# A linear-attention block with a low-rank mixer on one core: how the low-rank sum reaches its operand, and when U and V are converted

## The chip, the cores and the metric

The kernel runs as one program on one core of a Trainium2 chip. Times are device microseconds of one execution. Before the change three runs took 656.55, 654.02 and 652.91 us; the median is 654.02.

The engines are called as the profile calls them: PE (TensorE, with PEld for its weight loads), DVE (VectorE), ACT (ScalarE), POOL (GpSimd) and SP (SyncE, which here issues most transfers). Each engine works through its own queue in order.

## The reference, cut to what matters

Inputs q, k, v are [4, 8, 768, 64] (batch, heads, sequence, head width) in float32. U is [768, 32] and V is [32, 768], both float64, so their 64-bit words must be turned into float32 on the chip; the same holds for the two weight matrices (512 x 2048 and 2048 x 512).

```
for each block of the sequence:                      # per head, decay lam
    intra = (q k^T * Dmask) v
    inter = (q * lam_pow) kv_state
    out   = intra + inter
    kv_state = lam_block * kv_state + (k * rev_pow)^T v
x = out, heads side by side                          # [4, 768, 512]
h = x^T @ U @ V                                      # mixing along the sequence, rank 32
u = x + h^T
out = u + relu(u @ w_ch1) @ w_ch2
```

## The kernel before, in words

**The first stage** (about 0 to 115 us) goes through 24 steps, numbered s = 0 to 23: four batches of six blocks of 128 positions. Step s is in batch b = s // 6 at place c = s % 6. "First step" below means c = 0 (steps 6, 12, 18) and "second step" c = 1 (steps 7, 13, 19). In each step PE does, in this order: for step s+1 the transposes of q and k into the bank pqk (L361); the intra product of scores and values into px (L455); the state product into pkv (L427); the inter product into px (L466); and the scores of step s+1 into pss (L408). ACT copies the transposes out as `qt` and `kt` (L367) and px as x_nat (L472); it also scales the old state (faded, L401). DVE multiplies the scores by the decay mask (sm, L417) and forms the new state (kv, L433 to L438). POOL scales q and k (qs L392, ks L381). In steps 6 and 0 to 5 the state product comes ahead of the intra product. Its bank is pm up to step 6, pqk in a first or second step after that, and pss in the other steps: so in a second step it has to wait until ACT has copied `kt` out of pqk, and in the later steps the next scores have to wait until DVE has read pkv.

**The low-rank part.** In the last step of a batch, `low` (L477) multiplies U's transpose by the batch's x, in four column groups of 128, each into its own 32 rows of one bank: pp is [128, 128], 32 rows for each of four groups. The mixing product (`mix`, L567) needs this sum spread: its weights are 64 rows (32 of V's high part, 32 of V's low part) for each half of the columns, and so the moving operand p_hl needs the sum's high part and its low part, each twice, on both sets of 32 rows. V's own high and low parts lie in v_hl. In batches 0 to 2 the sum is taken out of pp as four 32x128 copies (ACT two, L492, and DVE two, L524) into a tile of 32 rows, DVE masks off the low bits (L527), ACT casts the high part to four places (L535, 32x256 each), POOL subtracts for the low part (L539, two of 32x256), and ACT copies that to the other rows (L546, two). These three parts are a list from which `next_of_low` (L550) runs the next one. In the first step of the next batch all three are run: two after the transposes, the third before the products. The last batch has its own form, which the change leaves alone.

From step 7 on, each step also mixes one earlier block (block s - 7; in a second step that is the first block of the batch before): `mix` on PE at the head of the step into the bank pm, `mixed` (L577) on DVE, which adds it to x_nat; SP stores the sum (u_d, L595). One step later `turn` (L597) transposes that block into the other half of pm, and `split` (L643) divides it into a high and a low part, on ACT (L644) and DVE (L645).

**Conversions.** `weight_steps` (L111) loads 64-bit words (L146) and makes float32 of them: `one` is two DVE operations, exponent (L166) and mantissa (L155, which with `apart` becomes a step of its own), and two ACT activations (L173, L174); `two` (L184), `three` (L192) and `four` (L197) are DVE. For weights, `five` is an ACT scaling (L215), `six` (L220) and `seven` (L227) are DVE. V's own last steps (L701) take the high part by a DVE mask (L718) and four ACT casts (L725) and the low part by DVE and POOL (L729). Where these steps run is set by hand, in a table of step numbers (L742); `aside` (L753) runs what the table has for a step, and what ACT has to do for it is run a little later, by `late`. The number NS stands for what is done around the first products of the next stage.

**The head of the products** (about 115 to 142 us): the first units of `hidden` (L823), 24 matmuls of 512 columns for each pair of column groups, with pieces of the last batch's mixing, sums (L575) and transposes (put, L608) put in by count (L892 to L904).

**The rest** (to 649.6 us) is the two large products, with PE in one row.

The order within a step is written out by hand as a list of pieces (L653 to L685); a program keeps that order on each engine and adds the waits.

Of the kernel before, what the change touches and what calls it, by code (L numbers as in the profile page):

```python
# [18 lines left out]
def kernel(  # L19
# [28 lines left out]
    nc = tc.nc  # L48
# [8 lines left out]
    R = moe_U.shape[1]  # L57
    G = P // R
# [45 lines left out]
    def tmp(name):  # L104
        return wconv.tile([P, C], FP32, tag="tmp", bufs=2, name=name)
# [129 lines left out]
    def w1_steps(ft, in_parts=False, apart=False):  # L235
        def tile_of():
            w1v[ft] = w1_pool.tile([P, 3, C], F32R, tag="w1", name="w1")
            return w1v[ft]

        cols = moe_w_ch1[:, ft * P : (ft + 1) * P].rearrange("(c p) f -> p c f", p=P)  # L240
        return split_steps(tile_of, cols, in_parts, apart=apart)
# [230 lines left out]
        nc.scalar.copy(xs[s].rearrange("p (a x e) -> p x a e", a=HP, x=2), px)  # L472
        del st[s]

    pps, others = {}, {}

    def low(b):  # L477

        pp = two_banks("pp", "px")[:, 0, 0:P] if b < B - 1 else bank([P, P], "pp", "b2")
        for c in range(NT):  # L480
            for g in range(G):
                nc.tensor.matmul(  # L482
                    out=pp[g * R : (g + 1) * R, :], lhsT=u_w[:, c, :],
                    rhs=xs[b * NT + c][:, g * P : (g + 1) * P],
                    start=(c == 0), stop=(c == NT - 1),
                )
        if b == B - 1:
            pps[b] = pp
            return
        pps[b] = rows_f = tmp("p_f")[0:R]  # L490
        for g in range(2):
            nc.scalar.copy(rows_f[:, g * P : (g + 1) * P], pp[g * R : (g + 1) * R])  # L492
        others[b] = pp

    def low_rows(b):

        pp, t = pps.pop(b), tmp("p_h")[0:R]
        own = [(slice(g * R, (g + 1) * R), slice(g * P, (g + 1) * P)) for g in range(G)]
        if b == B - 1:
            h, h2, l, l2 = (p_hl[g * R : (g + 1) * R] for g in range(G))  # L500
# [21 lines left out]
        rows_f, pp = pp, others.pop(b)  # L522
        for g in range(2, G):
            nc.vector.tensor_copy(  # L524
                out=rows_f[:, g * P : (g + 1) * P], in_=pp[g * R : (g + 1) * R]
            )
        nc.vector.tensor_scalar(t.bitcast(U32), rows_f.bitcast(U32), HI, None, ALU.bitwise_and)  # L527
        wide = [slice(x * 2 * P, (x + 1) * 2 * P) for x in range(2)]

        def place(g, low):  # L530
            return p_hl[g * R : (g + 1) * R, wide[low]]

        def spread():
            for g in range(G):
                nc.scalar.copy(place(g, 0), t[:, wide[g // 2]])  # L535

        def low_part():
            for x in range(2):
                nc.gpsimd.tensor_tensor(  # L539
                    out=place(2 * x, 1), in0=rows_f[:, wide[x]], in1=t[:, wide[x]],  # L540
                    op=ALU.subtract,
                )

        def spread_low():
            for x in range(2):
                nc.scalar.copy(place(2 * x + 1, 1), place(2 * x, 1).bitcast(FP32))  # L546

        pps[b] = [spread, low_part, spread_low]

    def next_of_low(b):  # L550
        pps[b].pop(0)()
# [102 lines left out]
    for s in range(NS):  # L654
        b, c = divmod(s, NT)
        done = s - NT - 1
        more = s + 1 < NS
        turns = done > 0 and (done - 1) // TG < FG
        mixes = 0 <= done < NS - NT - 1
        rows = c == 0 and b > 0  # L660
        step = [("fade", s)] * (c > 0)
        step += [("mix", done)] * mixes + [("turn", done - 1)] * turns
        step += [("split", done - 1)] * turns
        step += [("prep", s + 1)] * more
        step += [("mix", done + 1)] * (not more)
        step += [("next_of_low", b - 1)] * rows + [("next_of_low", b - 1)] * rows
        step += [("scale", s + 1)] * more
        step += [("mixed", done)] * mixes
        step += [("late", s - 1)] * (1 < s < NT - 1 or s > NT)
        step += [("turned", done - 2)] * (done > 1 and c == 1)  # L670
        step += [("mixed", done + 1)] * (not more)
        step += [("next_of_low", b - 1)] * rows
        both = [("intra", s), ("state", s)]
        step += (both if s > NT else both[::-1]) + [("next_v", s), ("inter", s)]
        step += [("late", s)] * (s < 2 or s in (NT - 1, NT))
        step += [("turned", done - 1)] * (done > 0 and c > 0)
        step += [("scores", s + 1)] * more
# [63 lines left out]
    )  # L741
    side = {}  # L742
    for steps, at in (
        (u_side, (-1, 1, 1, 2, 2)),
        (v_steps(), (0, 0, 3, 3, 4, 4, 4, 5, 5)),
        (w1_steps(0, True), (8, 9, 10, 11, 13, 14, 15, 16, 16, 17, 19)),
        (w1_steps(1, True, True), (15, 16, 17, 18, 20, 20, 21, 22, 23, 23, NS, NS)),
    ):
        assert len(steps) == len(at)
        for step, n in zip(steps, at):  # L750
            side.setdefault(n, []).append(step)

# [22 lines left out]
    load_next("k", nc.scalar)  # L775
    for name in "vkvq":
        load_next(name)
    aside(-1)
    load_next("k")
    make_identity(nc, ident)  # L780
    pl = two_banks("pl", "pss")[:, 0, 0:H]
# [122 lines left out]
        rest.append((unit, i, "turn", c0 + n))  # L904
    run["enter"] = enter_first_product
    head = [(pair, ft) for two in (pairs[:2], pairs[2:]) for ft in (0, 1) for pair in two]
    side = list(zip((0, 0), last)) + list(zip((0, 3, 3, 3, 4, 4, 4, 4), w1_steps(2)))
    for i, (pair, ft) in enumerate(head):
        before = {}
        for unit, n, *piece in rest:  # L910
# [162 lines left out]
```

## Time and profile before

| | |
|---|---|
| median of three runs | 654.02 us |
| the profiled execution | 651.42 us |
| its span, first to last instruction | 649.6 us |
| granted TensorE clock | 1.000 |
| PE busy in 0 to 33.79 us | 31.23 us |
| PE busy in 33.79 to 60.88 us | 26.56 us |
| PE busy in 60.88 to 89.60 us | 27.29 us |
| PE busy in 89.60 to 115.40 us | 24.83 us |
| PE busy in 115.40 to 145.00 us | 29.21 us |
| PE busy in 145.00 to 649.60 us | 500.78 us of 504.60 |

The four borders 33.79, 60.88, 89.60 and 115.40 are where `low` ends in batches 0, 1 and 2 and where the first product begins. A line of the timeline or of the waits gives the start and the length in us, the engine, the line of the kernel, the operation, the tile written and the tiles read, the shape, how many instructions are merged, and in brackets how long the engine was idle before and what released it. A wait for several things is put down to the one that came last by the record; where that one had long been done it was another.

### The profile page before, as it was taken

To read this page: it belongs to the slowest core of one execution; us is meant where nothing else is said; L and a number is where in the kernel's file an instruction comes from. 1 tells how busy PE (TensorE), PEld (TensorE's weight loads), DVE (VectorE), ACT (ScalarE), POOL (GpSimd) and SP (SyncE) were. 2 spreads that over 40 slices of the span, in tenths; PEclk is the share of its full clock that TensorE was granted. 3 is DMA by queue.
4 is the path that set the end of the run, shared out by engine and by line. 5 is a ranking of instruction groups with operands and counts; after the bars stand their busy time and mean duration, and the time that the engine had idled before them with its cause. 6 is when DMAs were issued, how large, how long until landed. Compare 5 with 4: busy or idle time off the path is not lost.

```text
span 649.6 us, 13396 instructions
## 1 busy us (share of the span) xinstructions
PE 639.9 (99%) x5242; PEld 538.1 (83%) x5242; DVE 441.2 (68%) x722; ACT 273.1 (42%) x506; POOL 116.4 (18%) x98
## 2 busy tenths in 40 slices
PE   8999999999999999999999999999999999999997
PEld 7889889788888888888888888888888888888886
DVE  6776879658997777777796254685575665755854
ACT  4676767435664444444454221332322322322320
POOL 4466868240000000000000000030030300300300
PEclk9999999999999999999999999999999999999999
DMA  9989994265876656566687999864363363453521
GB/s 229 247 200 251 231 252 124 77 216 167 290 256 227 211 210 211 210 211 211 210 292 267 321 324 399 285 216 147 97 227 98 115 211 97 160 164 98 178 82 65
DMA packets 131776, 131.29 MB, mean 202 GB/s; under 512 B 81346, under 2 KB 89794, under 8 KB 131714
## 3 DMA queue, kind: packets, MB, share of 16 engines
q1 hardware_dynamic: 106592, 124.02, 59.8%
q10 hardware_dynamic: 25122, 6.42, 4.4%
q8 instruction: 41, 0.67, 0.5%
q14 instruction: 21, 0.17, 0.1%
HBM read 80.09 MB, written 50.33 MB: 201 GB/s over the span
## 4 chain that ended last, share of the span: by engine, by line
PE 94%; ACT 2%; DVE 1%; DMA 1%; issue 1%; DVEq 0%; ACTq 0%
PE pz L837 26%; PE pz L971 13%; PE pz L969 13%; PE pd L973 13%; PE pd L848 13%; PE pss L408 3%; PE px L455 3%; PE px L466 2%; PE pqk L361 1%; PE pkv L427 1%; DMA qraw<-in_q_dram 1%; PE pp L482 1%; PE pm L567 1%; PE pm L630 1%; PE put L608 1%
## 5 line engine op out<-in xcount | busy, mean ns | idle before, releaser
L837 PE MATMUL pz<-u_hl,w 128*128 128x512 f32 x768 | 184.5, 390 | 0.0
L837 PEld LDWEIGHTS pz<-u_hl,w 128*128 128x128 f32 x768 | 143.6, 188 | 30.1 <-ACT r L844 0.3
L971 PE MATMUL pz<-w_hl,m 128*128 128x512 f32 x384 | 148.6, 389 | 0.0
L969 PE MATMUL pz<-w_hl,m 128*128 128x512 f32 x384 | 148.2, 389 | 0.0
L973 PE MATMUL pd<-w_d,m 128*128 128x512 f32 x384 | 147.4, 389 | 0.0
L952 ACT ACTIVATE m<-rm 128x512 fp32r<-128x512 f32 x96 | 60.6, 632 | 183.5 <-PE pd L973 123.0
L953 DVE SCALAR_TENSOR_TENSOR m<-rm,m 128x512 fp32r<-128x512 f32 x96 | 71.5, 747 | 96.0 <-ACT m L952 95.9
L998 POOL TENSOR_TENSOR o<-o,u 128x512 f32<-128x512 f32 x20 | 29.8, 1522 | 433.4 <-DVE o L994 433.4
L853 DVE SCALAR_TENSOR_TENSOR r<-pd,r 128x512 f32<-128x512 f32 x96 | 61.7, 685 | 60.1 <-ACT r L844 48.0
L848 PE MATMUL pd<-u_d,w 128*128 128x512 f32 x384 | 95.9, 390 | 0.0
L973 PEld LDWEIGHTS pd<-w_d,m 128*128 128x128 f32 x384 | 72.1, 188 | 15.3 <-DVE m L954 0.5
L971 PEld LDWEIGHTS pz<-w_hl,m 128*128 128x128 f32 x384 | 72.1, 188 | 15.0
L969 PEld LDWEIGHTS pz<-w_hl,m 128*128 128x128 f32 x384 | 72.1, 188 | 14.9
L848 PEld LDWEIGHTS pd<-u_d,w 128*128 128x128 f32 x384 | 71.8, 188 | 14.8
L844 ACT ACTIVATE r<-pz 128x512 f32<-128x512 f32 x96 | 51.8, 590 | 64.8 <-PE pz L837 64.8
L954 DVE SCALAR_TENSOR_TENSOR m<-m 128x512 fp32r<-128x512 f32 x96 | 74.7, 780 | 3.0
L417 DVE TENSOR_TENSOR sm<-pss,mask 128x512 f32<-128x512 f32 x48 | 30.9, 684 | 15.4 <-PE pss L408 15.2
L215 ACT ACTIVATE w<-wf 128x512 fp32r<-128x512 f32 x32 | 20.3, 634 | 35.7 <-DVE wf L197 27.4
L173 ACT ACTIVATE sc<-sc,ends 128x512 f32<-128x512 uint32 x30 | 21.6, 721 | 23.2 <-DVE sc L166 23.1
L455 PE MATMUL px<-vraw,sm 128*64 128x64 f32 x768 | 28.4, 225 | 2.7 <-ACT u_hl L644 0.9
L455 PEld LDWEIGHTS px<-vraw,sm 128*64 128x64 f32 x768 | 25.2, 137 | 4.7 <-issue 1.3
L408 PE MATMUL pss<-qt,kt 64*128 64x128 f32 x384 | 28.8, 290 | 0.1
(92 smaller groups left out, 619.4 us busy)
## 6 DMA issues: line engine op xcount, KB each, us to landing
r_d<-r SPq DMA_DIRECT2D x96, 256.0 KB, 2.6
rm<-r_d SPq DMA_DIRECT2D x96, 256.0 KB, 2.7
words<-in_moe_w_ch_dram SPq DMA_DIRECT2D x30, 512.0 KB, 4.4
w_d<-w SPq DMA_DIRECT2D x16, 768.0 KB, 3.4
w_hl<-w_d SPq DMA_DIRECT2D x16, 512.0 KB, 6.1
u_d<-x_nat SPq DMA_DIRECT2D x24, 256.0 KB, 4.0
u<-u_d SPq DMA_DIRECT2D x24, 256.0 KB, 4.2
qraw<-in_q_dram SPq DMA_DIRECT2D x23, 256.0 KB, 4.1
```

What stands on the lines that cost most here:

```text
L408: nc.tensor.matmul(out=pss[:, x, a, :], lhsT=kt[half[x], a, :], rhs=qt[half[x], a, :], start=True, stop=True,)
L455: nc.tensor.matmul(out=px[half[t], x, a, :], lhsT=sm[:, x, a, half[t]], rhs=vr[:, 2 * a + x, :], start=(a == 0), stop=(alone and a == HP - 1),
L837: nc.tensor.matmul(out=like(acc[g][0], g), lhsT=w[:, n, ct, :], rhs=columns(uhl[g][:, n], g, ct), start=(ct == 0 and n == 0), stop=(ct == ...
L844: nc.scalar.mul(rs[g], acc[g][0], 4096.0 + 1.0)
L848: nc.tensor.matmul(out=like(acc[g][1], g), lhsT=w[:, 2, ct, :], rhs=columns(ud[g], g, ct), start=(ct == 0), stop=(ct == CT - 1),)
L853: nc.vector.scalar_tensor_tensor(rs[g], acc[g][1], 4096.0, rs[g], ALU.mult, ALU.add)
L952: nc.scalar.activation(out=m[:, 0], in_=r, func=AF.Relu, scale=NEAR)
L953: nc.vector.scalar_tensor_tensor(m[:, 1], r, 0.0, hi, ALU.max, ALU.subtract)
L954: nc.vector.scalar_tensor_tensor(m[:, 2], hi, E, low, ALU.mult, ALU.subtract)
L969: nc.tensor.matmul(out=pz, lhsT=m[:, 0, cols], rhs=hl[:, 0], start=first, stop=False)
L971: nc.tensor.matmul(out=pz, lhsT=m[:, 1, cols], rhs=hl[:, 1], start=False, stop=end)
L973: nc.tensor.matmul(out=pd, lhsT=m[:, 2, cols], rhs=dd, start=first, stop=end)
```

## The change

The parts of the change, in the order of the code:

- In `low`, ACT takes the whole bank pp out with one 128x128 copy.
- The masks and the copies of DVE are gone for batches 0 to 2. The list of three parts is now: `own`, four ACT casts of 32x128 to the group's own rows, which round to the high part, with a POOL subtraction of 32x128 after each for the low part; `other(0)`, four ACT casts of 32x128 that bring the high parts to the other rows; `other(1)`, the same for the low parts.
- In a first step `own` runs after the transposes and `other(0)` after the inter product. In the following second step `other(1)` runs after the transposes.
- In a second step `mix` and `mixed` move from the head of the step to just ahead of the scores. On PE this product now stands behind the state and the inter product of that step.
- U's words are loaded in step 1 instead of ahead of the first step, V's in step 2 instead of step 0; their conversions run one to two steps later. V's high casts on ACT move from step 5 to step 6, behind `other(0)`.
- The first two weights' conversions move: the first is done in 12 steps with the mantissa apart, at other numbers of the table; of the second, the last four steps (`four` to `seven`) instead of two are done around the first units, three after the first and one after the second.

```diff
+        pps[b] = tmp("p_f")[:, 0:P]
+        nc.scalar.copy(pps[b], pp)
-        pps[b] = rows_f = tmp("p_f")[0:R]
-        for g in range(2):
-            nc.scalar.copy(rows_f[:, g * P : (g + 1) * P], pp[g * R : (g + 1) * R])
...
+        def place(g, of, low):
+            return p_hl[g * R : (g + 1) * R, low * 2 * P + (of % 2) * P :][:, 0:P]
+
+        def own():
             for g in range(G):
+                rows, at = pp[g * R : (g + 1) * R], place(g, g, 0)
+                nc.scalar.copy(at, rows)
                 nc.gpsimd.tensor_tensor(
+                    out=place(g, g, 1), in0=rows, in1=at.bitcast(FP32), op=ALU.subtract
                 )
+        def other(low):
+            for g in range(G):
+                nc.scalar.copy(place(g ^ 1, g, low), place(g, g, low).bitcast(FP32))
+
+        pps[b] = [own, lambda: other(0), lambda: other(1)]
...
-        step += [("mix", done)] * mixes + [("turn", done - 1)] * turns
+        step += [("mix", done)] * (mixes and c != 1) + [("turn", done - 1)] * turns
...
-        step += [("next_of_low", b - 1)] * rows + [("next_of_low", b - 1)] * rows
+        step += [("next_of_low", b - 1)] * (b > 0 and c < 2)
         step += [("scale", s + 1)] * more
-        step += [("mixed", done)] * mixes
+        step += [("mixed", done)] * (mixes and c != 1)
...
-        step += [("next_of_low", b - 1)] * rows
         both = [("intra", s), ("state", s)]
         step += (both if s > NT else both[::-1]) + [("next_v", s), ("inter", s)]
+        step += [("next_of_low", b - 1)] * rows
         step += [("late", s)] * (s < 2 or s in (NT - 1, NT))
         step += [("turned", done - 1)] * (done > 0 and c > 0)
+        step += [("mix", done), ("mixed", done)] * (mixes and c == 1)
         step += [("scores", s + 1)] * more
...
-        (u_side, (-1, 1, 1, 2, 2)),
-        (v_steps(), (0, 0, 3, 3, 4, 4, 4, 5, 5)),
-        (w1_steps(0, True), (8, 9, 10, 11, 13, 14, 15, 16, 16, 17, 19)),
-        (w1_steps(1, True, True), (15, 16, 17, 18, 20, 20, 21, 22, 23, 23, NS, NS)),
+        (u_side, (1, 3, 3, 4, 4)),
+        (v_steps(), (2, 2, 4, 4, 5, 5, 5, 6, 6)),
+        (w1_steps(0, True, True), (8, 9, 10, 11, 12, 14, 15, 16, 17, 17, 18, 20)),
+        (w1_steps(1, True, True), (15, 16, 17, 18, 21, 22, 23, 23, NS, NS, NS, NS)),
...
-    side = list(zip((0, 0), last)) + list(zip((0, 3, 3, 3, 4, 4, 4, 4), w1_steps(2)))
+    side = list(zip((0, 0, 0, 1), last)) + list(zip((0, 3, 3, 3, 4, 4, 4, 4), w1_steps(2)))
```

More of the change, by code (lines that the diff above doesn't have):

```diff
@@ L473, in inter @@
         del st[s]
-    pps, others = {}, {}
+    pps = {}
     def low(b):
@@ L489, in low @@
             return
-        pps[b] = rows_f = tmp("p_f")[0:R]
-        for g in range(2):
-            nc.scalar.copy(rows_f[:, g * P : (g + 1) * P], pp[g * R : (g + 1) * R])
-        others[b] = pp
+        pps[b] = tmp("p_f")[:, 0:P]
+        nc.scalar.copy(pps[b], pp)
     def low_rows(b):
-        pp, t = pps.pop(b), tmp("p_h")[0:R]
+        pp = pps.pop(b)
         own = [(slice(g * R, (g + 1) * R), slice(g * P, (g + 1) * P)) for g in range(G)]
         if b == B - 1:
+            t = tmp("p_h")[0:R]
             h, h2, l, l2 = (p_hl[g * R : (g + 1) * R] for g in range(G))
@@ L520, in low_rows @@
             return
[L522 to L533, printed above, removed]
+        def place(g, of, low):
+            return p_hl[g * R : (g + 1) * R, low * 2 * P + (of % 2) * P :][:, 0:P]
+        def own():
             for g in range(G):
-                nc.scalar.copy(place(g, 0), t[:, wide[g // 2]])
-        def low_part():
-            for x in range(2):
+                rows, at = pp[g * R : (g + 1) * R], place(g, g, 0)
+                nc.scalar.copy(at, rows)
                 nc.gpsimd.tensor_tensor(
-                    out=place(2 * x, 1), in0=rows_f[:, wide[x]], in1=t[:, wide[x]],
-                    op=ALU.subtract,
-                )
[L544 to L548, printed above, removed]
+                    out=place(g, g, 1), in0=rows, in1=at.bitcast(FP32), op=ALU.subtract
+                )
+        def other(low):
+            for g in range(G):
+                nc.scalar.copy(place(g ^ 1, g, low), place(g, g, low).bitcast(FP32))
+        pps[b] = [own, lambda: other(0), lambda: other(1)]
     def next_of_low(b):
@@ L777 @@
         load_next(name)
-    aside(-1)
     load_next("k")
```

## The prediction

> **What bounds the kernel now.** I read the page's busy shares and chain first, then the chain by stretches, then TensorE's gaps up to 145 us, and last the queues of ScalarE and VectorE around each gap.
>
> ```profile
> PE 639.9 (99%) x5242; PEld 538.1 (83%) x5242; DVE 441.2 (68%) x722; ACT 273.1 (42%) x506; POOL 116.4 (18%) x98
> PE 94%; ACT 2%; DVE 1%; DMA 1%; issue 1%; DVEq 0%; ACTq 0%
> ```
>
> TensorE (PE) is the bound: 94% of the chain. From 145 us on it is one unbroken row of products that the change leaves alone. An edit can gain only where PE waits before that, and cost only where it makes PE wait. These are the gaps near the edit (start, length, work, and in brackets the wait before it):
>
> ```profile
> 16.37 0.47 PE L361 MATMUL pqk<-ident,qraw 64*128 64x64 f32 x8 [0.44 <-DMA qraw<-in_q_dram]
> ...
> 40.29 0.69 PE L427 MATMUL pkv<-vraw,ks 128*64 128x64 f32 x16
> ...
> 72.26 1.24 PE L455 MATMUL px<-vraw,sm 128*64 128x64 f32 x32 [0.87 <-ACT qt L367]
> ...
> 104.94 1.24 PE L455 MATMUL px<-vraw,sm 128*64 128x64 f32 x32 [0.50 <-ACT u_hl L644]
> ```
>
> The first is a load that came late. The third and fourth are named after ScalarE, which had long been done; the late one is VectorE's mask product, behind two conversions:
>
> ```profile
> 70.05 1.51 DVE L155 TENSOR_SCALAR m<-words 128x512 uint32<-128x512 uint32 x1
> 71.47 1.28 DVE L417 TENSOR_TENSOR sm<-pss,mask 128x512 f32<-128x512 f32 x2
> ```
>
> The batch change is set by ScalarE (ACT). At step 18 to 19 its queue runs without a pause, and PE's state product `pkv` of the second step then waits for the copy `kt`, which frees its bank:
>
> ```profile
> 91.35 0.59 ACT L367 COPY kt<-pqk 128x512 f32<-128x512 f32 x1
> 91.83 1.66 ACT L535 CAST vp<-p_h 32x256 fp32r<-32x256 f32 x4
> 93.51 0.83 ACT L546 CAST vp<-vp 32x256 fp32r<-32x256 f32 x2
> 94.36 0.59 ACT L472 COPY x_nat<-px 128x512 f32<-128x512 f32 x1
> 95.06 0.60 ACT L644 ACTIVATE u_hl<-pm 128x512 fp32r<-128x512 f32 x1
> 95.61 0.58 ACT L367 COPY qt<-pqk 128x512 f32<-128x512 f32 x1
> 96.09 0.59 ACT L367 COPY kt<-pqk 128x512 f32<-128x512 f32 x1
> ...
> 96.73 0.55 PEld L427 LDWEIGHTS pkv<-vraw,ks 128*64 128x64 f32 x16 [0.27 <-ACT kt L367]
> ```
>
> That is the place the change rearranges: it takes VectorE out of the spreading and gives ScalarE more instructions ahead of that `kt`.
>
> **The price of a small copy.** By form, ScalarE's casts from SBUF take 403 ns (32x256, L535), 509 (32x384, L725) and 618 (32x512, L513), some 107 ns per 128 columns. A 32x128 one extrapolates to 0.30, and 0.31 from start to start. Bounds: 0.26, the 32x128 copy out of PSUM (L492, 256 ns), and 0.41, no cheaper than 256 columns. I take 0.31, the line through its own kind. Per batch ScalarE drops 0.52 + 1.66 + 0.83 = 3.0 us and gets one 128x128 copy (0.26 to 0.37, L492 and the 128x256 L367) and twelve of 0.31: 4.0 us. [...]
>
> **1. U's and V's words later.** One load ahead of q of the third step is gone, two behind it. SP issued U's words at 7.99 (0.85 us), so that q lands up to 0.85 earlier; the scores before the transposes end at 15.87, so the 0.44 wait goes and no more: -0.45. The wait of 0.40 at 11.95 stays, its load was issued at 6.97. Later both words are in the queues again, ahead of loads with three steps of lead; I give that nothing (if a load were late, up to the 0.44 back).
>
> **2. First batch change (steps 6 to 7).** ScalarE: `kt` ended at 35.60, now 35.15. Then the four own copies 1.2 (36.3), x_nat 0.55 (36.85), four others 1.2 (38.0), and V's four high casts, moved here from step 5, 2.07 (L725), so 40.1. `qt` and `kt` of step 8 follow, 0.48 apart: `kt` ends at 41.15, against 40.24. `pkv` starts at 41.2 against 40.29: +0.9. The mixing product was ahead of this wait and is now behind it: +0.27 (four matmuls of L567 in the chain). The third group of copies runs under `pkv` and the inter product (41.1 to 42.35, needed at 42.4). Step +1.2, part 1 already inside. VectorE, which held 0.59 + 0.42 + 1.55 us there, is free for `kv` and the mask at 36.6 when the scores end, so it is not the bound. Bounds: eight copies lie ahead of `kt`, so 0.26 gives +0.8 and 0.41 gives +2.0.
>
> **3. Second change (12 to 13), and w1's first conversion.** `kt` ends at 63.22. Own copies to 64.35, x_nat 64.9, others 66.1, u_hl 66.7, `qt` and `kt` to 67.7: `pkv` at 67.8 against 68.01, -0.2; the mixing product behind it +0.27: nothing. Then L166 and L155 (0.61 + 1.51) no longer stand before the mask of step 14, whose products waited 0.87. But the two exponent activations (1.46, L173 and L174) are now ahead of step 13's x_nat, 0.9 us late; behind it faded (1.07) and u_hl; VectorE's split and sum (two of 0.68) and `kv` wait for that, and the next scores for `kv`'s bank: they start at 74.25 against 74.58. Of the 0.87, 0.33 is kept, and mantissa and L184 (1.51, 1.36) in two successive steps take about half of that: -0.2. Bounds: copies of 0.26 give -0.5; copies of 0.41 give +0.6.
>
> **4. Third change (18 to 19).** `kt` 91.94, own copies to 93.1, the weight's L215 0.64 (its conversion is a step later) to 93.7, x_nat 94.25, others 95.5, u_hl 96.1, `kt` of step 20 to 97.1: `pkv` at 97.2 against 96.73, +0.45, and the mixing product +0.27: +0.7. VectorE's L220 waits for L215 and holds the mask to 95.4 or 96.2 (0.68 or 1.55, both in the trace); the intra product then ends at 96.6 or 97.3, no later than `kt`. Bounds: 0.26 gives +0.3, 0.41 with the long L220 +1.5.
>
> **5. Second weight.** Its exponents and mantissa part (steps 21 and 22): the mask behind L166 and L155 at 102 is free, -0.5 (0.3 to 0.6).
>
> **6. Head of the products.** Four of this weight's VectorE instructions move behind the first unit. After L853 (ends 126.94): L197 0.74, then L215 on ScalarE 0.63, then L220 0.68, to 129.1. The x_nat sum (L575, 128.18 to 128.86) queues behind, now to 129.75, and the transposes `put`, loading at 129.05, wait for it: +0.7. The weight itself is first used at 131.3, so it isn't late. Bounds: 0, if another queue were late anyway, and 1.0. SP's words fetch keeps its place.
>
> **Moved at no cost.** GpSimd's four subtractions replace two; the queries' scaling behind them (L392, 1.28) is needed at 41.8 and, at 0.5 to 0.8 a subtraction, done by 40. The store of u_d behind the later sum holds SP's next k load by some 4 us, two steps (8 us) ahead of need.
>
> **Sum.** +1.2 - 0.2 + 0.7 - 0.5 + 0.7 = +1.9 us; ends 0.8 - 0.5 + 0.3 - 0.6 + 0 = 0 and 2.0 + 0.6 + 1.5 - 0.3 + 1.0 = +4.8. The profiled execution is 651.42 us (span 649.6 and 1.8 around it) and would become 653.3; it lies 2.6 under the median of 654.02 (652.91 to 656.55), to which I add the same: 655.9.
>
> **Rivals.**
> *Small copies cost as much as large ones* (slower). If a 32x128 copy takes the 0.41 of a 32x256 one, the eight ahead of each `kt` add 0.8 three times: +4.3, 658.3. It decides from 3.3 us, that is 1.4 over the sum, 0.46 a change, copies of 0.36. For it: fixed time is most of these instructions (256 columns more cost 0.21 of 0.62). Against: the 0.256 of L492.
> *GpSimd is last at the first change* (no change). Four subtractions, L392 1.28, L381 1.1, V's low quarter 2.0 (L729): from 35.4 on, with 0.5 a subtraction, it ends at 41.8, before the mixing product's 42.4. At 0.8, as L539's mean of 806 ns for 256 columns, it ends at 43.0: +0.6, 656.5. [...]
> *The waits close and none opens* (faster). PE's waits in this stretch that the change touches: 0.44, 0.87, 0.50, twice 0.31 for `px` behind the copies of the low-rank sum, three times 0.27 for `pkv` behind `kt`, 1.3 for the mixing product behind ScalarE's casts (L567's weight loads, 0.9 and 0.4): -4.5, 649.5. It needs ScalarE not to be last at the batch changes, against 4.0 us of new copies for 3.0 of old.
>
> **How the numbers follow.** The sum 0.46 (own range 654.0 to 658.8), costly copies 0.30, GpSimd 0.12, closing waits 0.12. A measurement of this kernel tells about 0.5% (3.3 us) from no change: 650.75 and 657.29 are the borders. Above: 0.27 of the copies, 0.05 of the sum, 0.02 of GpSimd: 0.34. Below: 0.10 of the closing waits. Between: 0.56. Range 651.5 to 659.0.
>
> **What would show it.** After: `pkv` of steps 7, 13 and 19 waiting for `kt`, 3 us at the first; 32x128 casts of 0.30; the q wait at 16 us and the waits at 72 and 104 us gone; `put` in the second unit waiting 0.7 for the x_nat sum. I am wrong if the copies are far from 0.30, or if a load of batch 0 comes late behind the moved words.

## The result, and the profile after

The changed kernel takes 657.21 us (median of 14 runs, 654.13 to 659.01). The kernel before, run beside it on the same chips, takes 653.26 us (651.48 to 656.55, 14 runs). The ratio is 1.0047 with a 95% interval of 1.0032 to 1.0062: 3.1 us, where the two medians are 3.95 apart. The prediction was 655.9 us, 651.5 to 659.0, with no measurable change as the likeliest of the three signs: the time lies in the range, 1.3 us above the value, and the ratio lies inside the 0.5% that I called no change, close to its edge. The interval leaves out 1, so the kernel did become a little slower, and its upper end lies beyond that edge. Against the forecast of +1.9 us the change is 1.2 to 2.1 larger, and a good part of the loss has a cause that the prediction did not price.

The profiled execution is one of 657.99 us, with a span of 656.0. The shares of busy time on its page differ from those before by two points at most, and one digit of the clock's row is new: the first line is the busy time, the second the granted TensorE clock in forty slices of 16.4 us.

```profile
PE 641.7 (98%) x5242; PEld 540.6 (82%) x5242; DVE 432.7 (66%) x713; ACT 275.9 (42%) x521; POOL 117.0 (18%) x104
...
PEclk9979999999999999999999999999999999999999
```

The clock of the third slice is 0.7. Before, no slice was under full speed:

```profile
PEclk9999999999999999999999999999999999999999
```

The changed kernel by windows of 2 us around the first batch change (start and end, length, busy time and instructions of PE, PEld, DVE, ACT and POOL, then the granted clock, DMA share and GB/s):

```profile
38.00:40.00 2.00, 1.66 (x50) 1.54 (x46) 1.86 (x3) 1.93 (x6) 1.85 (x3) 1.00 0.99 220
40.00:42.00 2.00, 0.13 (x6) 0.00 (x0) 1.92 (x2) 1.94 (x5) 1.92 (x3) 0.90 0.53 121
42.00:44.00 2.00, 1.14 (x16) 1.04 (x16) 0.00 (x0) 1.90 (x6) 1.85 (x3) 0.50 0.00 0
44.00:46.00 2.00, 2.00 (x42) 1.86 (x42) 0.91 (x5) 0.80 (x3) 2.00 (x2) 0.50 0.31 73
46.00:48.00 2.00, 2.00 (x24) 2.00 (x24) 1.00 (x2) 0.90 (x4) 0.24 (x1) 0.50 0.53 140
48.00:50.00 2.00, 2.00 (x62) 1.93 (x60) 1.81 (x4) 1.52 (x3) 0.26 (x1) 0.89 0.78 193
```

PE stands from 40.1 to 42.86. The clock falls to half at about 41.7, still within the wait, and PE then works at half speed until 48.4. The timeline of PE over the same stretch shows the wait, and products that take 1.6 to 1.8 times their usual time:

```profile
42.86 1.23 PE L427 MATMUL pkv<-vraw,ks 128*64 128x64 f32 x16 [2.73 <-POOL vp L719]
44.02 1.13 PE L466 MATMUL px<-kv,qs 64*64 64x64 f32 x32
45.09 0.80 PE L556 MATMUL pm<-vp 64*128 64x256 f32 x4
45.68 1.91 PE L408 MATMUL pss<-qt,kt 64*128 64x128 f32 x16
```

The 16 matmuls of `pkv` take 1.23 where they took 0.69, those of the scores 1.91 where the same form takes 1.16 at 36.90. The releaser that the trace names, a GpSimd operation on V, is not the one: ScalarE's queue, from its own timeline, shows what `pkv` followed. (Lines are numbered here as in the changed kernel: L528 are the own casts, L535 those to the other rows, L715 V's high casts, L719 V's low part on GpSimd, L556 the mixing product. In e2, e5 and e12 the later lines are two higher; e4, e6 and e11 have the line numbers of the kernel before.)

```profile
36.47 0.61 ACT L528 CAST vp<-p_f 32x128 fp32r<-32x128 f32 x2
...
37.11 0.61 ACT L528 CAST vp<-p_f 32x128 fp32r<-32x128 f32 x2
37.75 0.59 ACT L472 COPY x_nat<-px 128x512 f32<-128x512 f32 x1
38.36 1.22 ACT L535 CAST vp<-vp 32x128 fp32r<-32x128 f32 x4
39.59 2.08 ACT L715 CAST vp<-vt 32x384 fp32r<-32x384 f32 x4
41.69 0.59 ACT L367 COPY qt<-pqk 128x512 f32<-128x512 f32 x1
42.17 0.59 ACT L367 COPY kt<-pqk 128x512 f32<-128x512 f32 x1
```

`kt` ends at 42.76 and `pkv` starts 0.10 later. This is the queue that the prediction wrote down: own copies, x_nat, other copies, V's four casts, `qt`, `kt`.

Where the time came from is read from the start of the scores in each step (L408 in the timelines), after against before:

| scores of step | before, us | after, us | difference |
|---|---|---|---|
| 3 | 19.19 | 19.46 | +0.27 |
| 7 | 36.26 | 36.90 | +0.64 |
| 9 | 45.85 | 51.16 | +5.31 |
| 12 | 58.27 | 63.56 | +5.29 |
| 15 | 74.58 | 79.79 | +5.21 |
| 18 | 86.99 | 93.12 | +6.13 |
| 20 | 97.97 | 104.89 | +6.92 |
| 22 | 107.26 | 113.59 | +6.33 |
| sixth `put` of the head | 136.14 | 142.84 | +6.70 |

So 4.67 of the 6.7 us were lost between step 7 and step 9, that is at the first batch change. The 0.92 from step 15 to 18 is behind no named wait: PE's timeline has two pauses of 0.20 and 0.23 within groups of matmuls there, and no other idle time that it names; other executions lose less there (e1, below: 0.16). This execution is worse than the median, and that of the kernel before was better than its own. The 14 runs explain part of the spread by their mean granted clocks: eight at 0.994 to 0.996 have a median of 657.55, four at 0.997 one of 655.95, and only two lie at 0.999 or 1.000 (654.13 and 657.65, so the clock is not the whole of the spread).

The waits of the second and third change in the timeline of PE:

```profile
73.39 0.69 PE L427 MATMUL pkv<-vraw,ks 128*64 128x64 f32 x16 [0.93 <-POOL ks L381]
...
79.79 1.13 PE L408 MATMUL pss<-qt,kt 64*128 64x128 f32 x15 [0.42 <-DVE kv L435]
...
101.29 1.24 PE L455 MATMUL px<-vraw,sm 128*64 128x64 f32 x32 [0.43 <-ACT vp L535]
...
103.30 0.69 PE L427 MATMUL pkv<-vraw,ks 128*64 128x64 f32 x16 [0.78 <-POOL ks L381]
```

The waits at 11.95, 16.37, 72.26 and 104.94 of the kernel before are gone.

### The profile page after: what moved, and what is told of

Same layout as the page of the kernel before. It is cut to its first block, busy times and chain, and to the rows that moved or that the text cites. A ratio compares the mean times of both kernels' runs of the same rounds, so it can differ in the third digit from the quotient of the medians.

```text
span 656.0 us, 13408 instructions
## 1 busy us (share of the span) xinstructions
PE 641.7 (98%) x5242; PEld 540.6 (82%) x5242; DVE 432.7 (66%) x713; ACT 275.9 (42%) x521; POOL 117.0 (18%) x104
## 4 chain that ended last, share of the span: by engine, by line
PE 93%; ACT 2%; DVE 1%; POOL 1%; issue 1%; DMA 1%; ACTq 0%; DVEq 0%; POOLq 0%
PE pz L826 26%; PE pz L960 13%; PE pz L958 13%; PE pd L962 13%; PE pd L837 13%; PE pss L408 4%; PE px L455 3%; PE px L466 2%; PE pkv L427 2%; PE pqk L361 1%; PE pp L482 1%; PE pm L556 1%; DMA kraw<-in_k_dram 1%; POOL ks L381 1%; PE pm L619 1%
## 5 line engine op out<-in xcount | busy, mean ns | idle before, releaser
L408 PE MATMUL pss<-qt,kt 64*128 64x128 f32 x384 | 29.7, 296 | 1.0 <-issue 0.5
L392 POOL TENSOR_TENSOR qs<-qt,powq 128x512 f32<-128x512 f32 x20 | 25.5, 1274 | 19.2 <-ACT qt L367 18.9
```

The source lines that it names most:

```text
L408: nc.tensor.matmul(out=pss[:, x, a, :], lhsT=kt[half[x], a, :], rhs=qt[half[x], a, :], start=True, stop=True,)
```

## The experiments

**Theory A**: the time is lost because V's four casts, now in step 6, stand ahead of `kt`, so that PE waits, and because the granted clock falls behind that wait; the low-rank sum's new way costs little. **Rival B**: the low-rank sum's new way costs by itself, at every batch change. **Rival C**: the later words hold back something at the start. (The expectations below have letters of their own, explained in each.) A fourth question came up on the way: what the new tables of the first two weights are worth.

Ratios are to the kernel before, run beside it on the same chip.

| run | us | ratio, 95% interval |
|---|---|---|
| e1, U and V as before | 653.53 | 1.0003 (0.9988 to 1.0018) |
| e2, 32 fillers in the wait | 656.94 | 1.0061 (1.0040 to 1.0082) |
| e3, weights as before | 660.73 | 1.0108 (1.0088 to 1.0129) |
| e4, before, U and V late | 655.49 | 1.0039 (1.0024 to 1.0054) |
| e5, 22 fillers | 655.25 | 1.0031 (1.0017 to 1.0045) |
| e6, before, weights spread | 651.87 | 0.9990 (0.9972 to 1.0007) |
| e8, low-rank part alone | 657.25 | 1.0063 (1.0042 to 1.0085) |
| e9, words a step later | 657.86 | 1.0072 (1.0050 to 1.0093) |
| e10, V's last steps in 5 | 656.0 | 1.0050 (1.0031 to 1.0069) |
| e11, e6 with late words | 657.3 | 1.0068 (1.0051 to 1.0084) |
| e12, 10 fillers | 654.44 | 1.0025 (1.0010 to 1.0040) |
| e13, late words, V early | 659.21 | 1.0103 (1.0085 to 1.0121) |

### e1: the changed kernel with U and V as before

```diff
-        (u_side, (1, 3, 3, 4, 4)),
-        (v_steps(), (2, 2, 4, 4, 5, 5, 5, 6, 6)),
+        (u_side, (-1, 1, 1, 2, 2)),
+        (v_steps(), (0, 0, 3, 3, 4, 4, 4, 5, 5)),
...
     for name in "vkvq":
         load_next(name)
+    aside(-1)
```

> The changed kernel with U's and V's loads and conversions put back where they were before. Theory A (V's four high casts on ScalarE, moved into step 6, hold `kt` of step 8 some 2 us, TensorE stands 2.7 us, and the granted clock is 0.5 for 5 us after it): no stretch with a clock of 0.5, the state product of step 7 starts within 1 us of the end of the intra product, and the kernel is as fast as before, 653.1 (652.0 to 654.5), a ratio of 0.998 to 1.002. Rival B (the twelve small copies a batch cost it, at all three batch changes): still 656 or more. Rival C (the loss is in the first weights' conversions): unchanged, 657.

Measured: 653.53 us, ratio 1.0003, all runs at a clock of 0.999 to 1.000. The wait for `kt` of step 7, which ends at 41.63, is 0.82:

```profile
41.73 0.69 PE L427 MATMUL pkv<-vraw,ks 128*64 128x64 f32 x16 [0.82 <-POOL qs L392]
```

From step 7 to 9 the difference to the kernel before grows by 0.44 (1.42 to 1.86). The whole loss of the changed kernel comes with U's and V's place in time, as theory A says; B alone can't explain it.

### e4: the kernel before with U and V late

```diff
-        (u_side, (-1, 1, 1, 2, 2)),
-        (v_steps(), (0, 0, 3, 3, 4, 4, 4, 5, 5)),
+        (u_side, (1, 3, 3, 4, 4)),
+        (v_steps(), (2, 2, 4, 4, 5, 5, 5, 6, 6)),
...
-    aside(-1)
```

> The kernel before with U's and V's loads and conversions at the later places, nothing else. Theory A: V's casts come behind the spreading and x_nat on ScalarE, the mixing product of step 7 is still ahead of that step's transposes and waits for them until about 40.4 us, TensorE stands some 3 us, the clock falls to 0.5; `pkv` of step 7 at 42.7 instead of 40.3, and 2.7 for the clock, less 0.45 at the start: 658 (656.5 to 659.5). Rival B: the small copies are not in it, so it is as before or a little faster, 652.8 to 653.3.

Measured: 655.49 us, ratio 1.0039, clocks of 0.994 to 0.997. So the late V costs 2.5 us without any of the low-rank part. That is under the 658 us that theory A gave it: the batch change lost 3.96 us where A had 5.1 (2.4 of wait and 2.7 of half speed), with half speed for 3.41 us and not for over 5, and the start gained 1.0 to 1.3 instead of 0.45. Here it is the mixing product that waits for V, and the clock falls behind it (timeline of PE, then the windows):

```profile
39.13 0.35 PE L567 MATMUL pm<-vp 64*128 64x256 f32 x1 [2.71 <-DVE vp L729]
39.90 0.50 PE L567 MATMUL pm<-vp 64*128 64x256 f32 x3 [0.41 <-POOL vp L729]
```

```profile
38.00:40.00 2.00, 0.45 (x3) 0.29 (x3) 1.94 (x3) 1.94 (x4) 1.85 (x3) 1.00 0.44 100
40.00:42.00 2.00, 2.00 (x35) 1.88 (x37) 0.95 (x2) 0.78 (x3) 1.14 (x2) 0.59 0.02 4
42.00:44.00 2.00, 2.00 (x46) 1.92 (x46) 0.02 (x1) 0.32 (x1) 1.25 (x1) 0.56 0.94 269
```

The start gains: no wait for q is left, and the scores of step 6 come 1.29 earlier than in the kernel before. The batch change takes 3.96 (from -1.00 at step 7 to +2.96 at step 8), after which the two kernels run in parallel to the head.

### e2, e5 and e12: TensorE kept at work in the wait

Small matmuls on a blank tile are put between the intra and the state product of step 7. In e2 the number is 16 (32 matmuls in the trace), in e5 11 (22), in e12 5 (10).

```diff
+        if s == NT + 1:
+            both.insert(1, ("keep_busy", 16))
         step += (both if s > NT else both[::-1]) + [("next_v", s), ("inter", s)]
```

> The changed kernel with 16 idle matmuls of 128x128 between the intra and the state product of step 7, which fill the wait on TensorE and compute nothing that is used. Theory A: `kt` of step 8 ends when it did, but the granted clock stays 1.00 from 40 to 50 us; the kernel gets back what half speed cost, 5.4 us at half, so 2.7: 654.5 (653.5 to 655.5), ratio about 1.002. If the wait alone were the loss and the clock only a mark in the record, the time stays 657.2, or rises where the fillers run past the end of `kt`.

> The changed kernel with 22 small matmuls (11 pairs, about 0.12 us each, 2.64 us in all) put between the intra and the state product of step 7, so that TensorE works in the wait for kt of 2.7 us and the fillers end when kt does. Theory A (the wait costs by the granted clock that falls to 0.5 behind it): the clock stays at 1.00, pkv starts within 0.3 us of the end of kt, and the 2.4 to 2.9 us that half speed took are given back: 654.3 to 655.0 us. Rival (the clock in the record follows something else, or the time lies in the wait itself): 657.2 us as the changed kernel.

> The changed kernel with 10 small matmuls (1.2 us) instead of 22 in the wait for kt in step 7, so that TensorE stands still for about 1.5 us of it. If the clock falls for any wait of more than about 1 us: half clock for 3.4 or 6.8 us and 656 to 657 us. If a stretch of 3.4 us has to be more than half idle: clock 1.00, 654.3 to 655.3 us as with 22.

Measured, e2: 656.94 us. The fillers took 3.84 us where the wait was 2.7, so `pkv` began 1.07 after `kt` was there; the clock stayed at 1.00. From step 7 to 9 it lost 3.31 against 4.67. The gain of 1.36 is about what full speed gives (2.33, from e5) less the 1.07, but two pauses of 0.73 and 1.21 within groups hide it in this execution's time. The median of its six runs, all at a clock of 0.999 or 1.000, is no better than the changed kernel's and misses theory A's 654.5; the late `pkv` explains 1.07 us of that and the rest stays open.

In e5 the fillers fit. PE's timeline:

```profile
39.27 2.72 PE L346 MATMUL idle<-blank 128*128 128x128 f32 x22
42.06 0.69 PE L427 MATMUL pkv<-vraw,ks 128*64 128x64 f32 x16
...
43.65 1.05 PE L408 MATMUL pss<-qt,kt 64*128 64x128 f32 x16
```

`kt` ended at 41.96 and `pkv` followed at 42.06, so the batch change is exactly as late as in the changed kernel; only the clock differs. From step 7 to 9 it loses 2.34 (-0.16 to +2.18), where the changed kernel lost 4.67: half speed cost 2.33. In e12, with 10 fillers, PE still waits 1.42 for `kt`, the clock is 1.00 as well, and the loss is again 2.34 (-1.10 to +1.24): its expectation that any wait over about 1 us lowers the clock falls. The other branch has the time right (654.3 to 655.3 expected, 654.44 measured); what it supposes, that a stretch of 3.4 us has to be more than half idle, is not shown by that.

```profile
38.33 1.38 PE L346 MATMUL idle<-blank 128*128 128x128 f32 x10
41.12 0.69 PE L427 MATMUL pkv<-vraw,ks 128*64 128x64 f32 x16 [1.42 <-POOL vp L721]
```

All 12 runs of each have clocks of 0.999 or 1.000. By the times, e12's ratio is 0.0022 under the changed kernel's (1.4 us) and e5's 0.0016 (1.0 us); the intervals overlap, and e5's time is a little above what theory A expected. The full 2.33 can't be expected from medians: half speed for 6.83 us, as in the trace, makes a mean clock of 0.995 over 656 us, and 3.41 us make 0.997, so by their mean clocks eight of the changed kernel's 14 runs had the long stretch, four a shorter one and two none. That is an estimate, since one of the 14 has a trace. That the fall of the clock costs is shown by the traces, and its size in the times agrees without being settled by them.

### e9, e10 and e13: V's casts back ahead of the batch change

Three tables were tried for late words with early casts. e9, then e10, then e13:

```diff
-        (u_side, (1, 3, 3, 4, 4)),
-        (v_steps(), (2, 2, 4, 4, 5, 5, 5, 6, 6)),
+        (u_side, (0, 1, 1, 2, 2)),
+        (v_steps(), (1, 1, 3, 3, 4, 4, 4, 5, 5)),
```

```diff
-        (v_steps(), (2, 2, 4, 4, 5, 5, 5, 6, 6)),
+        (v_steps(), (2, 2, 4, 4, 5, 5, 5, 5, 5)),
```

```diff
-        (u_side, (1, 3, 3, 4, 4)),
-        (v_steps(), (2, 2, 4, 4, 5, 5, 5, 6, 6)),
+        (u_side, (0, 3, 3, 3, 3)),
+        (v_steps(), (1, 1, 3, 3, 4, 4, 4, 5, 5)),
```

> The changed kernel with U's and V's words loaded one step later than before (not ahead of the first step's loads) and V's four high casts back in step 5, ahead of the batch change. Theory A (in the changed kernel only V's casts in step 6 cost, the later loads themselves gain 0.4 to 1.0 us at the start): the wait for kt in step 7 is under 1 us, the clock stays at 1.00, 652.5 to 653.2 us. Rival B (the words in the queues behind the first loads hold back a later load): 653.5 to 654.5. Rival C (the clock falls whatever stands in step 6): 657.

> The changed kernel with one thing undone: V's last two steps (the mask, four high casts on ScalarE, the low part) stand in step 5 again and not in step 6; the words are loaded as late as in the changed kernel. Theory A (V's casts ahead of kt in step 6 make the 2.7 us wait and with it the half clock, and nothing else of the later words costs): in step 7 PE waits under 1.2 us, the clock stays at 1.00, 652.6 to 653.6 us. Rival B (the casts only move the wait to step 6, where the low-rank sum then waits behind them): 654.5 to 656. Rival C (the later words cost at the start): a wait before step 5 of more than 1 us, 655 or more.

> The changed kernel with U's words loaded in step 0 and converted in step 3 (three steps after the load, so that VectorE does not stand for them), V's words loaded in step 1, and V's conversion at its old step numbers, so that its four high casts are done ahead of the first batch change. Theory A (only V's casts ahead of kt cost, with the half clock behind them): from step 7 to step 9 at most 1 us is lost against the kernel before, the clock stays at 1.00, no wait over 1 us before step 7, 652.3 to 653.5 us. Rival B (whatever is later than in the kernel before costs somewhere: four of U's and two of V's operations in step 3 hold the mask of step 3 or 4): a wait of 1 us or more there, 654.5 or more.

All three missed theory A's time, each for its own reason.

e9, 657.86 us: VectorE's first operation on U's words stands in its queue ahead of the mask of step 3, and the words land only at 20.8. VectorE waits 6.01 us, PE 4.79 behind it, and the clock falls to 0.5 for 6.83 us:

```profile
20.80 0.26 DVE L166 TENSOR_SCALAR sc<-words 128x192 uint32<-128x192 uint32 x1 [6.01 <-DMA words<-in_moe_U_dram]
```

```profile
22.37 1.98 PE L455 MATMUL px<-vraw,sm 128*64 128x64 f32 x32 [4.79 <-DVE sm L417]
```

Neither rival said this. Rival B had the words hold back another load, for some 1 us; here U's own words are wanted too early, and 7.2 us are lost by step 4, half speed included. The batch change, though, answers the question: with V's casts ahead of it, it costs 0.44 from step 7 to 9 (+6.49 to +6.93), against 4.67.

e10, 656.0 us: the edit did not do what I meant. Moving the last two entries from 6 to 5 moves V's mask and low part on VectorE and GpSimd, but the four casts still run on ScalarE behind `other(0)`:

```profile
37.38 1.22 ACT L535 CAST vp<-vp 32x128 fp32r<-32x128 f32 x4
38.61 2.07 ACT L715 CAST vp<-vt 32x384 fp32r<-32x384 f32 x4
40.71 0.59 ACT L367 COPY qt<-pqk 128x512 f32<-128x512 f32 x1
41.19 0.59 ACT L367 COPY kt<-pqk 128x512 f32<-128x512 f32 x1
```

So the time at the edge of its rival B is no support for that rival. The run settles something else:

```profile
35.09 2.57 POOL L719 TENSOR_TENSOR vp<-vf,vt 32x384 fp32r<-32x384 f32 x2 [4.24 <-DVE vt L708]
```

```profile
41.88 0.75 PE L427 MATMUL pkv<-vraw,ks 128*64 128x64 f32 x16 [2.57 <-POOL qs L392]
```

GpSimd was done with V at 37.7, and `pkv` still waited 2.57, until 0.10 after the end of `kt` at 41.78 as in the changed kernel: GpSimd's work on V, which the trace names there, is not the cause. The half speed lasted 3.42 us here instead of 6.83, and the loss from step 7 to 9 is 3.69 instead of 4.67.

e13, 659.21 us (U's third conversion step is issued here ahead of ScalarE's two activations that it needs, so that U's values are not the reference's; instructions and sizes are the same): it lost 7.01 us by step 5, as its rival B had it in kind, but not through words that came late. V's words were issued at 16.0 and 16.9 and took at most 7.2 us to land. VectorE's first operation on them starts at 27.50, right after ScalarE's second activation on U's exponents, which works in the same buffer `sc`:

```profile
27.01 0.46 ACT L174 ACTIVATE sc<-sc,vp 128x192 uint32<-128x192 f32 x1
```

```profile
27.50 1.21 DVE L166 TENSOR_SCALAR sc<-words 64x384 uint32<-64x384 uint32 x1 [1.90 <-DMA kraw<-in_k_dram]
```

That wait, and three operations on V's words behind it (the last is L184, 1.37), delay the mask of step 5:

```profile
31.12 1.98 PE L455 MATMUL px<-vraw,sm 128*64 128x64 f32 x32 [5.05 <-DVE sm L417]
```

The batch change costs 0.45 (+6.64 to +7.09). Four kernels with the new low-rank part and V's casts ahead of the change (e1, e9, e13 and e8 below) thus agree on 0.44 to 0.45, and the two with the casts in it, PE waiting or filled up to `kt`, and a full clock (e5, e12) on 2.34. What of rival C is true: words whose first use stands in VectorE's queue before they land (e9) hold the mask, and so does a conversion that has to wait for ScalarE (e13); both cost more than the batch change did. The changed kernel's own tables avoid both.

### e3, e6 and e8: the first two weights' tables

e3 is the changed kernel with the weights' tables of the kernel before, e8 has in addition U and V as before, so that only the low-rank part of the change, with the mixing product's new place, is left. e6 is the kernel before with smaller steps for the two weights and nothing else.

```diff
-        (w1_steps(0, True, True), (8, 9, 10, 11, 12, 14, 15, 16, 17, 17, 18, 20)),
-        (w1_steps(1, True, True), (15, 16, 17, 18, 21, 22, 23, 23, NS, NS, NS, NS)),
+        (w1_steps(0, True), (8, 9, 10, 11, 13, 14, 15, 16, 16, 17, 19)),
+        (w1_steps(1, True, True), (15, 16, 17, 18, 20, 20, 21, 22, 23, 23, NS, NS)),
...
-    side = list(zip((0, 0, 0, 1), last)) + list(zip((0, 3, 3, 3, 4, 4, 4, 4), w1_steps(2)))
+    side = list(zip((0, 0), last)) + list(zip((0, 3, 3, 3, 4, 4, 4, 4), w1_steps(2)))
```

```diff
-        (w1_steps(0, True), (8, 9, 10, 11, 13, 14, 15, 16, 16, 17, 19)),
-        (w1_steps(1, True, True), (15, 16, 17, 18, 20, 20, 21, 22, 23, 23, NS, NS)),
+        (w1_steps(0, True, True), (8, 9, 10, 11, 13, 14, 15, 16, 16, 16, 17, 19)),
+        (w1_steps(1, True, True), (15, 16, 17, 18, 20, 21, 22, 23, 23, 23, NS, NS)),
```

> The changed kernel with the two first weights' conversions at the places of before, the rest of the change kept. Theory A: the wait for the mask in step 20 to 21 returns (+0.5), the one in step 14 returns (+0.2 to +0.9), the wait of the transposes in the second unit goes (-0.35): 657.5 to 658.3, no faster than the changed kernel. Rival C (the second weight's later steps behind the first units are the loss): 655 or less. B says nothing here, unchanged.

> The kernel before, with only the first two weights' conversions in smaller steps (mantissa apart from the exponent in both, no two of them in step 20, nothing moved to the first units). Theory A (two waits of TensorE behind the mask products at 72 and 104 us are what the old tables cost): both waits shrink or go, -0.5 to -1.4 us, 651.6 to 652.5. Rival (another queue is late next, as in the changed kernel's steps 15 to 18): 653.0 to 653.6, the kernel before.

> The kernel before, with only the low-rank sum's new way and the mixing product's new place in a second step; all conversions as before. Theory A (the first two batch changes cost about nothing, the third 0.7 us, and the mask of step 14 comes late behind the mantissa as in the run with the old tables of the weights, 1.8 us of wait and up to 2 us of half clock): 654.5 to 657.0. Rival B (the late mask came from U's and V's words): 653 to 654. Rival C (the new low-rank part alone is faster, since VectorE is out of the spreading): under 652.5.

Measured: e8 657.25 us, ratio 1.0063; e3 660.73, 1.0108, slower than either theory had it. The expectation of e8 had named the late mask and the half clock behind it; the time is 0.25 above its range. The new low-rank part alone is slower by 4.1 us, and the first batch change takes little of that: +0.44 from step 7 to 9 in e8. The time goes at step 14. The timelines of VectorE and of PE in e8:

```profile
72.70 0.69 DVE L568 TENSOR_TENSOR x_nat<-pm,x_nat 128x512 f32<-128x512 f32 x1 [0.23 <-PE pm L556]
73.31 0.93 DVE L166 TENSOR_SCALAR sc<-words 128x512 uint32<-128x512 uint32 x1
74.16 1.48 DVE L155 TENSOR_SCALAR m<-words 128x512 uint32<-128x512 uint32 x1
75.57 1.27 DVE L417 TENSOR_TENSOR sm<-pss,mask 128x512 f32<-128x512 f32 x2
```

```profile
76.35 1.67 PE L455 MATMUL px<-vraw,sm 128*64 128x64 f32 x32 [1.65 <-ACT kt L367]
```

With the mixing product moved behind the inter product, `mixed` (L568) runs late in step 13, and the two conversions of the weight come behind it, directly ahead of the mask of step 14. The 0.87 of wait in the kernel before became 1.65 here and 1.81 in e3, and in both the clock fell to 0.5 for 3.41 us. From step 13 to 15 e8 loses 2.68 and e3 3.09, and around steps 20 to 22 both lose more waits for the mask (in e8 0.71 and 0.86). Moving the weights' conversions, which I had priced as a gain of 0.5 us in the second weight and a part of the 0.2 of the second change, is worth 3.5 to 4.0 us once the low-rank part is there (e3 to the changed kernel, e8 to e1). So rival B is half right: the new low-rank part costs by itself, but in step 14, by what stands behind it in VectorE's queue. In the kernel before, smaller steps for the two weights (not quite the same tables) are worth about 0.6: e6, ratio 0.9990, an interval that holds 1, so that no gain is shown by the times. In e6's trace the waits at 72.26 and 104.94 are gone, one of 0.48 for the mask has come at 88, and the sum from step 13 to 22 is -0.75.

### e11: the best of both, as I thought

```diff
-        (u_side, (-1, 1, 1, 2, 2)),
-        (v_steps(), (0, 0, 3, 3, 4, 4, 4, 5, 5)),
+        (u_side, (1, 3, 3, 4, 4)),
+        (v_steps(), (2, 2, 4, 4, 5, 5, 5, 5, 5)),
...
-    aside(-1)
```

This is on top of e6's two lines.

> The kernel before with the two edits that the runs so far point to: the first two weights' conversions in smaller steps, and U's and V's words loaded as late as in the changed kernel but V's casts kept in step 5; the low-rank sum and the mixing product as before. Theory A (the two waits behind the mask go, -0.7, and the start gains 0.4 to 1.0 of the later loads): 650.9 to 651.6 us. Rival (V's parts, now all in step 5, are late for the mixing product of step 7 as in the run with the old low-rank part and the late words): a wait of 1 us or more at 39 us, 652.5 or more.

Measured: 657.3 us. The rival was right, and the wait larger than it said:

```profile
41.89 1.39 PE L567 MATMUL pm<-vp 64*128 64x256 f32 x4 [5.49 <-ACT vp L725]
```

GpSimd works on V's low part (2.56 us) before the low-rank sum's; ScalarE waits 3.03 for it, and V's casts, behind that, run from 41.33 to 43.4. No version here beats the kernel before by more than its interval; e6 is the nearest.

## Why the prediction was right, and where its steps were not

**The price of a small copy** (0.30, 0.31 from start to start) was right. By form:

```profile
L535 ACT CAST vp<-vp 32x128 fp32r<-32x128 f32 x24 | 7.1, 296 | 0.6
...
L528 ACT CAST vp<-p_f 32x128 fp32r<-32x128 f32 x12 | 3.5, 294 | 0.2
...
L491 ACT COPY p_f<-pp 128x128 f32<-128x128 f32 x3 | 0.8, 267 | 4.7 <-PE pp L482 4.7
```

With it the rival of costly copies (0.41, 658.3 us) falls, although its time is near the measured one.

**Step 1, the later words, -0.45**: the mechanism was right, its size is not settled. Both waits for q go, not only the one at 16.37 (I had the one at 11.95 stay); in e4 and e12, the scores of step 6 come 1.29 and 1.21 earlier. But in the eight kernels with these late words the scores of step 7 lie between 1.10 earlier and 0.76 later than before. In the profiled execution of the changed kernel k's first load landed late (waits of 0.43 and 0.76 at 5.21 and 6.66) and hides it. e5 and e10 show a late k of 0.34 and 0.30, e12 none, with the same loads: it differs between executions.

**Step 2, the first batch change, +1.2**: this is the step that failed. The wait itself was right, 3 us predicted and 2.73 measured, with the queue of ScalarE as written (6.0 us from one `kt` to the next predicted, 6.17 measured). The term as predicted is +1.65 from step 7 to 9 once the start's -0.45 is taken out; at full clock it is 2.34 (e5, e12). Of the 0.7 between them, 0.35 is that the first step's `kt` came later against PE's scores than before, 0.17 the longer queue, and some 0.1 the mixing product behind `pkv`. On top of that came 2.33 of half speed (the changed kernel against e5), which no term held. I priced a wait by its length alone. The experiments put the length itself down to V's casts: with these ahead of the batch change, and the same twelve small copies in place, the step costs 0.44.

**Step 3, second change, -0.2**: -0.08 from step 12 to 15, and -0.16 in e1. The wait of 0.93 for `kt` and the 0.42 of the scores behind `kv` were foreseen. What was mis-sized is what the edit avoids: without the moved conversions, steps 13 to 15 cost 2.7 us and more (e8, e3). I had compared only with the kernel before, whose waits don't stay when `mixed` moves.

**Step 4, third change, +0.7**: +0.79 from step 18 to 20, the same in e1 and 0.78 in e5. Right.

**Step 5, second weight, -0.5**: -0.59 from step 20 to 22, and -0.58 in e5. Right.

**Step 6, head, +0.7**: +0.37 from the first unit to the sixth `put`, and 0.36 in e1, about half of the term. The `put` waits for the x_nat sum as said, but for 0.16.

**GpSimd last at the first change**: falls, narrowly. Its subtractions took 2.02 us for four, 0.5 each; of the 0.5 to 0.8 in the prediction no run of the kernel before shows the lower value (L539 takes 0.81 for 256 columns). At full clock (e5) it ends with V's low part at 43.11, and the mixing product starts at 43.30 without a wait. **The waits close**: those of 0.44, 0.87 and 0.50 did close, and new ones of 2.73, 0.93, 0.78 and 0.42 came. The first three are waits for ScalarE at the batch changes, the reason given against this rival, though at the first change V's casts weigh more than the copies.

The steps 3 to 6 sum to +0.5 against +0.7 predicted. What stays above that is the first batch change. The sum was +1.9, the measured change 3.1 by the ratio and 3.95 by the medians. Half speed gives 1.7 of it on the mean, if eight of fourteen executions lost 2.33 and four 1.35 (an estimate: e10's 3.69 less the 2.34); the larger step 2 gives 0.7, and the steps 3 to 6 take 0.2 back. These terms come to 4.1; the start, whose size differs between executions, has to make up the rest, which no run here singles out. That the value of 655.9 is only 1.3 from the measured time is in part luck: it was counted from three runs of the kernel before, whose median of 654.02 lies 0.76 above that of fourteen.

## What to carry to other kernels

When a wait on TensorE grows, look at the granted clock behind it: here it stayed at 1.00 behind a wait of 1.42 us (e12) and fell to 0.5 behind one of 1.65 (e8), and at the first batch change the price was the wait and nearly as much again for half speed (2.34 and 2.33 us). An edit that moves one reader in an engine's queue moves what stands behind it (in e8 the mask of step 14 behind `mixed`, and PE waits 1.65 us), so price the old tables against the new order and not only against the kernel before: here moving the weights' conversions was worth perhaps 0.6 us by itself (not clear of the noise) and 3.5 to 4.0 with the rest. And before a conversion is put later, look for which queue it stands in at the time that its data land: the later words gained up to 1 us at the start and lost 2.3 to 4.7 at the place where V's casts came to stand.

## What the runs showed of the hardware that I had not expected

The half-speed stretches seen here come in two lengths only, read in windows of 0.2 us:

| kernel | longest wait of PE there, us | half speed for, us |
|---|---|---|
| e1 | 0.82 | none |
| e12 | 1.42 | none |
| e8 | 1.65 | 3.41 |
| e3, step 14 | 1.81 | 3.41 |
| e10 | 2.57 | 3.42 |
| e4 | 2.71 | 3.41 |
| e3, step 7 | 2.72 | 6.83 |
| after | 2.73 | 6.83 |
| e9 | 4.79 | 6.83 |
| e13 | 5.05 | 6.83 |
| e11 | 5.49 | 6.83 |

The longer stretch, 6.83, is twice the shorter, 3.41 or 3.42. The shortest wait of the table with half speed behind it is 1.65 us (e8), the longest without it 1.42 (e12). The length of a wait alone does not decide: e6 has a pause of 2.28 us at 25 to 27 with a clock of 1.00 (0.999 on the mean of that execution), and nearly equal waits of 2.71 (e4) and 2.72 (e3) are followed by one length and by two. What else decides is not shown by these runs.

Such pauses are the second thing. Within groups of matmuls that have no named wait PE stood for 0.2 to 2.3 us, at other places in other executions. e6 in PE's timeline:

```profile
27.39 0.40 PE L361 MATMUL pqk<-ident,kraw 64*128 64x64 f32 x7 [2.28 <-issue]
```

The same place has 1.26 in e8, 0.35 in e1 and none before. They make single profiles of this kernel differ by up to 2 us for no reason that the profile shows, which is why steps were compared one by one here. Their cause stays open.
